# Re-ordering the head of a one-core kernel: x tile 0 in two loads, weights ahead of x tile 2, copies in halves, and the filler matmuls re-cut

## The chip, the cores and the metric

The kernel runs on one core of a Trainium2 chip. The metric is the device time in microseconds (us) of one execution; lower is better. A run's *span*, from the first to the last instruction in the trace, is about 1.4 us shorter than its time. One of the runs of the kernel before took 2341 us and is left out everywhere. The experiments ran in three groups of four on three different chips (a1 to b1, c1 to c4, d1 to d4), each beside runs of the kernel before on the same chip.

PE is the matmul engine (PEld its weight loads), DVE is VectorE, ACT ScalarE, POOL GpSimd, SP the engine that issues most loads. In these traces each engine executes its instructions in the order in which the program gives them to it, and one that waits holds up those behind it.

## The reference, cut to what matters

```python
xn = layernorm(x)                       # x: 2048 x 1024
h  = xn @ w1 + b1                       # 1024 -> 3584
act = h * tanh(softplus(h))
y_B = act @ w2                          # 3584 -> 1024
# y_A: a diagonal complex recurrence over the 2048 rows:
# projection in (B), scan, projection out (C), skip (Dskip)
return x + y_A + y_B
```

The kernel handles 2048 rows in four blocks of 512, each of four *x tiles* of 128 rows. Nothing can be multiplied before x is normalised and transposed. In the first block that is done tile by tile: statistics, square root, scaling, transposes on PE into PSUM (the banks to which PE writes its results), copies from PSUM into `xnT`. Then the first six output tiles of the dense layer are computed in two halves of 256 rows (`first_half`), so that PE can start when only tiles 0 and 1 are ready. Everything up to there is "the head" below.

## The kernel before

The parts that the change and the argument touch. First the loads and their order; ring slots are 512 KB pieces of `w1`, in pieces of 512 bytes:

```python
for q in range(NQ):
    load_x(SP, 0, q)                      # four x tiles, 256 KB each
for src, r0, n in ((A_log_dt, ...), (A_Lambda_im, ...), (A_Lambda_re, ...), (B_b1, ...)):
    AC.dma(... st[r0:r0 + n, :] ...)      # the parameters: 13 KB in four small loads, ScalarE's queue
for i in range(NRING):
    ring_load()                           # weights, SP's queue
    if i == 3:
        SP.dma(... dsk ...)
```

Then the head itself. `keep_busy` issues filler matmuls whose result nobody reads; they are there for the PE clock.

```python
keep_busy(76)
for q in range(2):                        # VectorE: statistics of tiles 0 and 1
    first_sums_v(q, 0); first_sums_v(q, 1); first_var_v(q)
first_sqrt(0)                             # ScalarE
first_mean_a(2)                           # ScalarE: sums of tile 2, ahead of tile 1's root
first_sqrt(1)
first_var_a(2); first_sqrt(2)
first_apply(0); first_transpose(0); keep_busy(4)
first_apply(1); first_transpose(1); keep_busy(4)
first_copy(0, VE)
first_copy(1, VE, 0, 4); first_copy(1, AC, 4, NK)
# ... tile 3's sums and root on ScalarE, first_apply(2), first_apply(3) ...
for f in range(NSPLIT):
    first_half(f, 0)
    if f == 0:                            # the parameter transpose, and its copy
        PE.op(... transpose(ps16(5)[:, 0:NST], st[:, :], ident[0:NST, 0:NST]) ...)
        vop(... tensor_copy(par[:, :], ps16(5)[:, 0:NST]) ...)
    if f in (2, 3):
        first_transpose(f); first_copy(f, VE)
```

Of the kernel before, what the change touches and what calls it, by code (L numbers as in the profile page):

```python
# [5 lines left out]
ALU = mybir.AluOpType  # L6
# [3 lines left out]
P = 128  # L10
# [146 lines left out]
def build_kernel(nc, A_x, A_Lambda_re, A_Lambda_im, A_B_re, A_B_im, A_C_re, A_C_im,  # L157
                 A_log_dt, A_Dskip, B_w1, B_b1, B_w2, out):
    bf16, f32, i32 = DT.bfloat16, DT.float32, DT.int32
    S, D = A_x.shape[1], A_x.shape[2]  # L160
# [4 lines left out]
    NQ = TB // P  # L165
    NK = D // P
# [8 lines left out]
    PE = Queue(nc, "pe")  # L175
    VE = Queue(nc, "ve")
    AC = Queue(nc, "ac")
    PO = Queue(nc, "po")
    SP = Queue(nc, "sp")

    def sb(name, shape, dtype):
        return nc.alloc_sbuf_tensor(name, shape, dtype)
# [4 lines left out]
    b_ring = [Buf("ring%d" % i) for i in range(NRING)]  # L187
# [16 lines left out]
    b_xnT = [Buf("xnT%d" % q, parts=[Buf("xnT%d_%d" % (q, h)) for h in range(2)]) for q in range(NQ)]  # L204
# [3 lines left out]
    xx = sb("xx", [P, 2, NQ, D], bf16)  # L208
    b_xx = [[Buf("xx%d_%d" % (i, q), parts=[Buf("xx%d_%d_%d" % (i, q, h)) for h in range(2)])
             for q in range(NQ)] for i in range(2)]  # L210
# [7 lines left out]
    NST = 3 * NJ + NF  # L218
    st = sb("st", [NST, P], bf16)
    b_st = Buf("st")  # L220
    ident = sb("ident", [P, P], bf16)
    b_ident = Buf("ident")
    par = sb("par", [P, NST], f32)
    b_par = Buf("par")
    stats = sb("stats", [P, 2, 2, 6], f32)
    b_stats = [Buf("stats%d" % i) for i in range(2)]
# [21 lines left out]
    ps = nc.alloc_psum_tensor("ps", [P, 8, TB], f32)  # L248
    b_ps = [Buf("ps%d" % i) for i in range(8)]

    def ps16(i):
        return ps[:, i, :].bitcast(bf16)
# [23 lines left out]
    vop, aop, pop = VE.op, AC.op, PO.op  # L276
# [7 lines left out]
    def load_x(queue, blk, q):  # L284
        r0 = blk * TB + q * P
        i = blk % 2
        queue.dma(lambda e: e.dma_start(xx[:, i, q, :], A_x[0, r0:r0 + P, :]),  # L287
                  s_xx[i][q] if blk else s_x0[q], writes=[b_xx[i][q]])

    for q in range(NQ):  # L290
        load_x(SP, 0, q)
    for src, r0, n in ((A_log_dt, 2 * NJ, NJ), (A_Lambda_im, NJ, NJ), (A_Lambda_re, 0, NJ),
                       (B_b1, 3 * NJ, NF)):
        AC.dma(lambda e, src=src, r0=r0, n=n: e.dma_start(
# [8 lines left out]
    def ring_load():  # L303
        i = n_loaded[0]
        if i >= len(items):
            return
        n_loaded[0] += 1
        kind, g = items[i]
        s = i % NRING
        if kind == "w1":  # L310
            dst = ring[:, s, :].rearrange("p (k f) -> p k f", k=NK)
            src = B_w1[:, g * 256:(g + 1) * 256].rearrange("(k p) f -> p k f", p=P)
        else:
            dst = ring[:, s, :].rearrange("p (f d) -> p f d", f=2)
            src = B_w2[g * 256:(g + 1) * 256, :].rearrange("(f p) d -> p f d", p=P)
        SP.dma(lambda e: e.dma_start(dst, src), s_ring[s], writes=[b_ring[s]])

    for i in range(NRING):
        ring_load()
        if i == 3:  # L320
            SP.dma(lambda e: e.dma_start(dsk[:], A_Dskip.partition_broadcast(P)), s_dsk, writes=[b_dsk])


# [12 lines left out]
    def rc(q, n):  # L336
        return rs[:, q, n:n + 1]

    def first_sums_v(q, h):
        s = q % 2  # L340
        vop(lambda e: e.bn_stats(stats[:, s, h, :], xx[:, 0, q, h * 512:(h + 1) * 512]),
            reads=[b_xx[0][q]], writes=[b_stats[s]])

    def first_var_v(q):
        s = q % 2
        vop(lambda e: e.bn_aggr(mv[:, q, :], stats[:, s, :, :]), reads=[b_stats[s]], writes=[b_mv[q]])

    def first_mean_a(q):
        aop(lambda e: e.activation(sq[:], xx[:, 0, q, :], AF.Identity, bias=kon[:, 1:2], accum_out=rc(q, 3)),
            reads=[b_xx[0][q], b_kon], writes=[b_sq, b_rs[q]])  # L350
        aop(lambda e: e.activation(mv[:, q, 0:1], rc(q, 3), AF.Copy, scale=-1.0 / D),
            reads=[b_rs[q]], writes=[b_mv[q]])

    def first_var_a(q):
        aop(lambda e: e.activation(sq[:], xx[:, 0, q, :], AF.Square, bias=mv[:, q, 0:1], accum_out=mv[:, q, 1:2]),
            reads=[b_xx[0][q], b_mv[q]], writes=[b_sq, b_mv[q]])

    def first_sqrt(q):
        scale = 1.0 if q < 2 else 1.0 / D
        aop(lambda e: e.activation(rc(q, 1), mv[:, q, 1:2], AF.Sqrt, scale=scale, bias=kon[:, 2:3]),  # L360
            reads=[b_mv[q], b_kon], writes=[b_rs1[q]])

    def first_apply(q):
        y = rc(q, 1)
        vop(lambda e: e.reciprocal(y, y), reads=[b_rs1[q]], writes=[b_rs1[q]])
        vop(lambda e: e.tensor_scalar(xn[:, q, :], xx[:, 0, q, :], mv[:, q, 0:1], y,
                                      op0=ALU.subtract if q < 2 else ALU.add, op1=ALU.mult),
            reads=[b_xx[0][q], b_mv[q], b_rs1[q]], writes=[b_xn[q]])

    def bank_T(q, k):  # L370
        if q == 1 and k >= NK // 2:
            return 5
        return 6 + q % 2

    def first_transpose(q):
        for k in range(NK):
            bank = bank_T(q, k)
            PE.mm(lambda e, k=k, bank=bank: e.transpose(ps16(bank)[:, k * P:(k + 1) * P],  # L378
                                                        xn[:, q, k * P:(k + 1) * P], ident[:]),
                  reads=[b_xn[q], b_ident], writes=[b_ps[bank]],  # L380
                  first=k == 0 or bank != bank_T(q, k - 1), last=k == NK - 1 or bank != bank_T(q, k + 1))

    def first_copy(q, queue, k0=0, k1=NK):
        dst = xnT[:, k0:k1, q * P:(q + 1) * P]
        bank = bank_T(q, k0)
        srcp = ps16(bank).rearrange("p (k t) -> p k t", k=NK)[:, k0:k1, :]
        b_dst = b_xnT[q] if k1 - k0 == NK else b_xnT[q].parts[k0 // 4]
        if queue is AC:
            aop(lambda e: e.copy(dst, srcp), reads=[b_ps[bank]], writes=[b_dst])  # L389
        else:  # L390
            vop(lambda e: e.tensor_copy(dst, srcp), reads=[b_ps[bank]], writes=[b_dst])
# [62 lines left out]

    def keep_busy(n):
        for i in range(n):
            PE.mm(lambda e: e.matmul(ps[:, 4, 0:P], lhsT=ident[:], rhs=ident[:], start=True, stop=True),  # L457
                  reads=[b_ident], writes=[b_ps[4]], first=i == 0, last=i == n - 1)

    keep_busy(76)  # L460
    aop(lambda e: e.activation(rs[:, :, 3], kon[:, 2:3].to_broadcast([P, NQ]), AF.Sqrt), reads=[b_kon], writes=b_rs)
    for q in range(2):
        first_sums_v(q, 0)
        first_sums_v(q, 1)
        first_var_v(q)
    first_sqrt(0)
    first_mean_a(2)
    first_sqrt(1)
    first_var_a(2)
    first_sqrt(2)  # L470
    first_apply(0)
    first_transpose(0)
    keep_busy(4)
    first_apply(1)
    first_transpose(1)
    keep_busy(4)
    first_copy(0, VE)
    first_copy(1, VE, 0, 4)
    first_copy(1, AC, 4, NK)
    first_mean_a(3)  # L480
    first_var_a(3)
    first_sqrt(3)
    first_apply(2)
    first_apply(3)
    NSPLIT = 6

    def first_half(f, half):
        s, fi = f // 2, f % 2
        wt = ring[:, s, :].rearrange("p (k f) -> p k f", k=NK)
        ts = slice(half * 256, half * 256 + 256)  # L490
        for k in range(NK):
            PE.mm(lambda e, k=k: e.matmul(ps[:, f, ts], lhsT=wt[:, k, fi * P:(fi + 1) * P], rhs=xnT[:, k, ts],  # L492
                                          start=k == 0, stop=k == NK - 1),
                  reads=[b_ring[s]] + b_xnT[2 * half:2 * half + 2], writes=[b_ps[f]],
                  first=half == 0 and k == 0, last=half == 1 and k == NK - 1)

    for f in range(NSPLIT):
        first_half(f, 0)
        if f == 0:
            PE.op(lambda e: e.transpose(ps16(5)[:, 0:NST], st[:, :], ident[0:NST, 0:NST]),  # L500
                  reads=[b_st, b_ident], writes=[b_ps[5]])
            vop(lambda e: e.tensor_copy(par[:, :], ps16(5)[:, 0:NST]), reads=[b_ps[5]], writes=[b_par])
        if f in (2, 3):
            q = f
            first_transpose(q)
            first_copy(q, VE)

# [345 lines left out]
```

## Time and profile before

| | before |
|---|---|
| first three runs | 623.45, 623.82 us (and the one of 2341 us) |
| span of the profiled run | 622.6 us |
| PE busy | 617.8 us, 99% |
| first real matmul | 10.40 us |
| first 512-column matmul (the head is over) | 21.90 us (its weight load) |
| PE's waits after the first real matmul | 0.3 us in one |

The page of the kernel before, its first line of engine times and the two lines of the chain of waits that ended last (share of the span by engine, then by line):

```profile
PE 617.8 (99%) x2981; PEld 289.3 (46%) x2981; DVE 464.5 (75%) x684; ACT 246.7 (40%) x162; POOL 50.2 (8%) x47
...
PE 99%; DVE 0%; ACT 0%; POOL 0%; issue 0%; POOLq 0%
PE ps L715 48%; PE ps L638 29%; PE ps L658 18%; PE ps L492 2%; PE ps L457 1%; DVE mt L663 0%; PE ps L378 0%; DVE xx L752 0%; ACT xnT L389 0%; POOL ident L325 0%; POOL ident L324 0%; PE ps L500 0%; POOL kon L328 0%; POOLq L838 0%
```

PE is the limit. L457 is the filler, L378 the transposes, L492 the split sums, L500 the parameter transpose. A matmul record's busy time says little of its rate, as matmuls overlap (a filler record lasts 0.22 us, and the next starts 0.06 us after it); what counts is the start of one against the start of the next.

The list of waits of PE, whole kernel (who waited for whom: total us, times, longest):

```profile
PE ps L457 <- POOL kon L328: 1.4, 1, 1.4
PE ps L492 <- ACT xnT L389: 0.5, 1, 0.5
PE ps L715 <- DVE mt L663: 0.3, 1, 0.3
```

After 10.4 us PE waits once, for 0.3 us by this list. So a shorter head should shift everything behind it, and nothing else in the kernel is to be had this way.

The timeline of the head before (start, duration, engine, line, operation, count; in brackets the idle time before and what ended it):

```profile
1.41 7.11 PE L457 MATMUL ps<-ident 128*128 128x128 bf16 x76 [1.41 <-POOL kon L328]
...
3.65 1.42 DVE L341 BATCH_NORM_STATS2 stats<-xx 128x6 f32<-128x512 bf16 x2 [3.65 <-DMA xx<-in_A_x_dram]
...
5.78 1.15 ACT L349 ACTIVATE sq<-xx,kon 128x1024 bf16<-128x1024 bf16 x1
...
6.91 0.55 DVE L366 TENSOR_SCALAR xn<-xx,mv,rs 128x1024 bf16<-128x1024 bf16 x1
...
7.67 0.55 DVE L366 TENSOR_SCALAR xn<-xx,mv,rs 128x1024 bf16<-128x1024 bf16 x1
...
8.36 0.61 PE L378 MATMUL ps<-ident,xn 128*128 128x128 bf16 x8
...
10.40 1.03 PE L492 MATMUL ps<-xnT,ring 128*128 128x256 bf16 x8 [0.54 <-ACT xnT L389]
11.37 0.20 PE L500 MATMUL ps<-ident,st 52*128 52x52 bf16 x1
```

Tile 0 is normalised at 7.46 us, but PE is in its filler until 8.36. The filler's starts lie 107 ns apart up to 7.05 us and 56 ns from there on: the clock was released (went from half rate to full) at about 7.1 us. The parameter transpose stands behind eight real matmuls, at 11.37 us; the trace's landing records have the last parameter at 5.38 us, so it had 6 us to spare.

### The profile page before, as it was taken

Reading aid. Unit: us, or ns where it says so; the run is one execution under the profiler, and the core shown is the slowest. Engines: PE = TensorE matmul, PEld = TensorE weight load, DVE = VectorE, ACT = ScalarE, POOL = GpSimd, SP = SyncE. Lnnn points to the kernel's source line nnn. Section 1 sums busy time; section 2 is a strip of 40 time slices with the busy share of each in tenths; the row PEclk is TensorE's granted clock in tenths of the full one; section 3 lists DMA queues with packets and bytes.
Section 4 is the critical chain, followed back from the end, with each engine's and each line's share of the span. In section 5 each row is a group of like instructions: output and inputs, shape, how many; then the busy total and the mean of one; then the engine's idle time right before and its main releaser. Section 6 shows DMA issues by size and latency. Waiting matters only on the chain.

```text
span 622.6 us, 7430 instructions
## 1 busy us (share of the span) xinstructions
PE 617.8 (99%) x2981; PEld 289.3 (46%) x2981; DVE 464.5 (75%) x684; ACT 246.7 (40%) x162; POOL 50.2 (8%) x47
## 2 busy tenths in 40 slices
PE   8999999999999999999999999999999999999998
PEld 8644444444444444444444444444444444444443
DVE  4799999999557599998047759999624856999603
ACT  6679996332069950000008992000000999000000
POOL 1899000000100000000010000000000000000000
DMA  9999976750364400864055420285204541033001
GB/s 265 230 274 272 221 142 187 192 164 1 123 188 161 136 0 18 228 172 125 17 186 148 157 103 0 76 222 158 87 34 136 156 149 68 0 126 111 1 0 68
DMA packets 124188, 79.41 MB, mean 128 GB/s; under 512 B 48890, under 2 KB 106490, under 8 KB 124154
## 3 DMA queue, kind: packets, MB, share of 16 engines
q1 hardware_dynamic: 120656, 71.58, 42.2%
q10 hardware_dynamic: 2538, 4.21, 1.8%
q0 software_dynamic: 960, 3.15, 1.6%
q8 instruction: 24, 0.39, 0.3%
q14 instruction: 10, 0.08, 0.0%
HBM read 63.19 MB, written 4.19 MB: 108 GB/s over the span
## 4 chain that ended last, share of the span: by engine, by line
PE 99%; DVE 0%; ACT 0%; POOL 0%; issue 0%; POOLq 0%
PE ps L715 48%; PE ps L638 29%; PE ps L658 18%; PE ps L492 2%; PE ps L457 1%; DVE mt L663 0%; PE ps L378 0%; DVE xx L752 0%; ACT xnT L389 0%; POOL ident L325 0%; POOL ident L324 0%; PE ps L500 0%; POOL kon L328 0%; POOLq L838 0%
## 5 line engine op out<-in xcount | busy, mean ns | idle before, releaser
L715 PE MATMUL ps<-ring,act 128*128 128x512 bf16 x896 | 194.2, 379 | 0.3 <-DVE mt L663 0.3
L638 PE MATMUL ps<-xnT,ring 128*128 128x512 bf16 x848 | 183.7, 379 | 0.0
L616 ACT ACTIVATE act<-hb 128x3584 bf16<-128x3584 bf16 x16 | 50.9, 3183 | 245.5 <-DVE hb L645 245.0
L715 PEld LDWEIGHTS ps<-ring,act 128*128 128x128 bf16 x896 | 87.6, 98 | 106.3 <-DVE mt L663 0.8
L638 PEld LDWEIGHTS ps<-xnT,ring 128*128 128x128 bf16 x848 | 83.0, 98 | 99.8
L645 DVE TENSOR_SCALAR hb<-ps,par 128x512 bf16<-128x512 f32 x112 | 82.9, 748 | 56.2 <-PE ps L638 54.3
L715 PE MATMUL ps<-CT,hT 128*128 128x512 bf16 x512 | 111.2, 379 | 0.0
L658 PE MATMUL ps<-xnT,BT 128*128 128x512 bf16 x512 | 111.2, 379 | 0.0
L663 DVE TENSOR_TENSOR mt<-ps,tab 128x1024 bf16<-128x1024 f32 x64 | 75.4, 1220 | 13.3 <-PE ps L658 11.7
L715 PEld LDWEIGHTS ps<-CT,hT 128*128 128x128 bf16 x512 | 50.1, 98 | 60.4
L658 PEld LDWEIGHTS ps<-xnT,BT 128*128 128x128 bf16 x512 | 50.1, 98 | 60.4
L752 DVE TENSOR_TENSOR xx<-ps,xx 128x1024 bf16<-128x1024 f32 (+1 forms) x17 | 19.5, 1161 | 70.1 <-PE ps L715 70.0
L681 DVE TENSOR_TENSOR_SCAN hT<-cs,qi,hT 128x512 bf16<-128x512 f32 x48 | 58.9, 1270 | 0.0
L618 ACT ACTIVATE act<-act 128x3584 bf16<-128x3584 bf16 x16 | 51.0, 3191 | 0.2
L617 ACT ACTIVATE act<-act 128x3584 bf16<-128x3584 bf16 x16 | 51.0, 3190 | 0.2
L686 DVE TENSOR_TENSOR mt<-hT,tab 128x1024 bf16<-128x1024 bf16 x64 | 41.4, 689 | 1.1
L623 DVE TENSOR_TENSOR act<-act,hb 128x3584 bf16<-128x3584 bf16 x16 | 32.9, 2059 | 1.3 <-ACT act L618 1.3
L287 POOL DMA_DIRECT2D xx<-in_A_x_dram x12 | 6.7, 558 | 254.0 <-DVE xx L752 250.1
L592 ACT ACTIVATE ct<-CT,cs 128x512 f32<-128x512 bf16 x16 | 11.5, 718 | 28.8 <-DVE CT L594 24.5
L617 ACT ACT_TABLE_LOAD x16 | 20.5, 1283 | 0.3
L618 ACT ACT_TABLE_LOAD x16 | 20.5, 1283 | 0.3
L681 DVE TENSOR_TENSOR_SCAN hT<-cs,hT 128x512 bf16<-128x512 f32 x16 | 18.7, 1209 | 0.0
(78 smaller groups left out, 280.4 us busy)
## 6 DMA issues: line engine op xcount, KB each, us to landing
ring<-in_B_w_dram SPq DMA_DIRECT2D x112, 512.0 KB, 3.7
out_dram<-xx ACTq DMA_DIRECT2D x15, 256.0 KB, 2.0
xx<-in_A_x_dram POOLq DMA_DIRECT2D x12, 256.0 KB, 4.2
xx<-in_A_x_dram SPq DMA_DIRECT2D x4, 256.0 KB, 3.5
dsk<-in_A_Dskip_dram SPq DMA_DIRECT2D x1, 256.0 KB, 6.3
out_dram<-xx ACTq DMA_DIRECT2D x2, 128.0 KB, 1.7
xnT<-xn SPq DMA_TRANSPOSE x12, 4.5
BT<-in_A_B_re_dram SPq DMA_TRANSPOSE x8, 5.7
```

The lines of the kernel that those rows point to most:

```text
L616: aop(lambda e: e.activation(a, hs, AF.Exp), reads=[b_hb[g % 2]], writes=[b_act[g]])
L617: aop(lambda e: e.activation(a, a, AF.Ln, bias=1.0), reads=[b_act[g]], writes=[b_act[g]])
L618: aop(lambda e: e.activation(a, a, AF.Tanh), reads=[b_act[g]], writes=[b_act[g]])
L623: vop(lambda e: e.tensor_tensor(a, a, hs, op=ALU.mult), reads=[b_act[g], b_hb[g % 2]], writes=[b_act[g]])
L638: PE.mm(lambda e, k=k: e.matmul(ps[:, bank, :], lhsT=wt[:, k, fi * P:(fi + 1) * P], rhs=xnT[:, k, :], start=k == 0, stop=k == NK - 1), rea ...
L645: vop(lambda e: e.tensor_scalar(hb[:, hs, :], ps[:, bank, :], b1(f), None, op0=ALU.add), reads=[b_ps[bank], b_par], writes=[b_hbf[hs]])
L658: PE.mm(lambda e, j=j, ci=ci, k=k, bank=bank: e.matmul(ps[:, bank + ci, :], lhsT=BT[:, ci, j, k, :], rhs=xnT[:, k, :], start=k == 0, stop= ...
L663: vop(lambda e, s=s, u=u, j=j: e.tensor_tensor(mt[:, s, :, :], u, tab[:, s, j, :].unsqueeze(1).to_broadcast([P, 2, TB]), op=ALU.mult), rea ...
L681: vop(lambda e, ci=ci, init=init: e.tensor_tensor_scan(out=hT[:, ci, j, :], data0=cj("r", j).to_broadcast([P, TB]), data1=hT[:, ci, j, :], ...
L686: vop(lambda e, s=s: e.tensor_tensor(mt[:, s, :, :], hT[:, :, j, :], tab[:, s, j, :].unsqueeze(1).to_broadcast([P, 2, TB]), op=ALU.mult), ...
L715: PE.mm(lambda e: e.matmul(ps[:, u, :], lhsT=lhsT, rhs=rhs, start=st_, stop=last), reads=reads, writes=[b_ps[u]], first=st_, last=last)
L752: vop(lambda e: e.tensor_tensor(xr, src, xr, op=ALU.add), reads=b_src + [b_x], writes=[b_x])
```

## The change

The intent is to start the first real matmul sooner: tile 0 in two loads so that statistics start on the first half; the first weights ahead of x tiles 2 and 3; tile 2's statistics moved from ScalarE to VectorE so that nothing stands before tile 1's root; copies of both tiles in halves on two engines out of four PSUM banks; and less filler, with the parameter transpose put into it.

```diff
--- before.py
+++ after.py
@@ -287,8 +287,10 @@
         queue.dma(lambda e: e.dma_start(xx[:, i, q, :], A_x[0, r0:r0 + P, :]),
                   s_xx[i][q] if blk else s_x0[q], writes=[b_xx[i][q]])
 
-    for q in range(NQ):
-        load_x(SP, 0, q)
+    for h in range(2):
+        SP.dma(lambda e, h=h: e.dma_start(xx[:, 0, 0, h * 512:(h + 1) * 512], A_x[0, 0:P, h * 512:(h + 1) * 512]),
+               DmaSem(nc, "d_x00_%d" % h), writes=[b_xx[0][0].parts[h]])
+    load_x(SP, 0, 1)
     for src, r0, n in ((A_log_dt, 2 * NJ, NJ), (A_Lambda_im, NJ, NJ), (A_Lambda_re, 0, NJ),
                        (B_b1, 3 * NJ, NF)):
         AC.dma(lambda e, src=src, r0=r0, n=n: e.dma_start(
@@ -317,7 +319,10 @@
 
     for i in range(NRING):
         ring_load()
-        if i == 3:
+        if i == 0:
+            load_x(SP, 0, 2)
+            load_x(SP, 0, 3)
+        if i == 5:
             SP.dma(lambda e: e.dma_start(dsk[:], A_Dskip.partition_broadcast(P)), s_dsk, writes=[b_dsk])
 
 
@@ -339,7 +344,7 @@
     def first_sums_v(q, h):
         s = q % 2
         vop(lambda e: e.bn_stats(stats[:, s, h, :], xx[:, 0, q, h * 512:(h + 1) * 512]),
-            reads=[b_xx[0][q]], writes=[b_stats[s]])
+            reads=[b_xx[0][q].parts[h]], writes=[b_stats[s]])
 
     def first_var_v(q):
         s = q % 2
@@ -356,7 +361,7 @@
             reads=[b_xx[0][q], b_mv[q]], writes=[b_sq, b_mv[q]])
 
     def first_sqrt(q):
-        scale = 1.0 if q < 2 else 1.0 / D
+        scale = 1.0 if q < 3 else 1.0 / D
         aop(lambda e: e.activation(rc(q, 1), mv[:, q, 1:2], AF.Sqrt, scale=scale, bias=kon[:, 2:3]),
             reads=[b_mv[q], b_kon], writes=[b_rs1[q]])
 
@@ -364,12 +369,12 @@
         y = rc(q, 1)
         vop(lambda e: e.reciprocal(y, y), reads=[b_rs1[q]], writes=[b_rs1[q]])
         vop(lambda e: e.tensor_scalar(xn[:, q, :], xx[:, 0, q, :], mv[:, q, 0:1], y,
-                                      op0=ALU.subtract if q < 2 else ALU.add, op1=ALU.mult),
+                                      op0=ALU.subtract if q < 3 else ALU.add, op1=ALU.mult),
             reads=[b_xx[0][q], b_mv[q], b_rs1[q]], writes=[b_xn[q]])
 
     def bank_T(q, k):
-        if q == 1 and k >= NK // 2:
-            return 5
+        if q < 2 and k >= NK // 2:
+            return 4 + q
         return 6 + q % 2
 
     def first_transpose(q):
@@ -454,30 +459,35 @@
 
     def keep_busy(n):
         for i in range(n):
-            PE.mm(lambda e: e.matmul(ps[:, 4, 0:P], lhsT=ident[:], rhs=ident[:], start=True, stop=True),
-                  reads=[b_ident], writes=[b_ps[4]], first=i == 0, last=i == n - 1)
-
-    keep_busy(76)
+            PE.mm(lambda e: e.matmul(ps[:, 3, 0:P], lhsT=ident[:], rhs=ident[:], start=True, stop=True),
+                  reads=[b_ident], writes=[b_ps[3]], first=i == 0, last=i == n - 1)
+
+    keep_busy(44)
     aop(lambda e: e.activation(rs[:, :, 3], kon[:, 2:3].to_broadcast([P, NQ]), AF.Sqrt), reads=[b_kon], writes=b_rs)
+    PE.op(lambda e: e.transpose(ps16(2)[:, 0:NST], st[:, :], ident[0:NST, 0:NST]),
+          reads=[b_st, b_ident], writes=[b_ps[2]])
+    keep_busy(12)
     for q in range(2):
         first_sums_v(q, 0)
         first_sums_v(q, 1)
         first_var_v(q)
-    first_sqrt(0)
-    first_mean_a(2)
-    first_sqrt(1)
-    first_var_a(2)
-    first_sqrt(2)
+        first_sqrt(q)
     first_apply(0)
     first_transpose(0)
     keep_busy(4)
     first_apply(1)
     first_transpose(1)
     keep_busy(4)
-    first_copy(0, VE)
+    first_copy(0, VE, 0, 4)
     first_copy(1, VE, 0, 4)
+    first_copy(0, AC, 4, NK)
     first_copy(1, AC, 4, NK)
     first_mean_a(3)
+    vop(lambda e: e.tensor_copy(par[:, :], ps16(2)[:, 0:NST]), reads=[b_ps[2]], writes=[b_par])
+    for h in range(2):
+        first_sums_v(2, h)
+    first_var_v(2)
+    first_sqrt(2)
     first_var_a(3)
     first_sqrt(3)
     first_apply(2)
@@ -491,17 +501,13 @@
         for k in range(NK):
             PE.mm(lambda e, k=k: e.matmul(ps[:, f, ts], lhsT=wt[:, k, fi * P:(fi + 1) * P], rhs=xnT[:, k, ts],
                                           start=k == 0, stop=k == NK - 1),
-                  reads=[b_ring[s]] + b_xnT[2 * half:2 * half + 2], writes=[b_ps[f]],
+                  reads=[b_ring[s]] + [b.parts[k // 4] for b in b_xnT[2 * half:2 * half + 2]], writes=[b_ps[f]],
                   first=half == 0 and k == 0, last=half == 1 and k == NK - 1)
 
     for f in range(NSPLIT):
         first_half(f, 0)
-        if f == 0:
-            PE.op(lambda e: e.transpose(ps16(5)[:, 0:NST], st[:, :], ident[0:NST, 0:NST]),
-                  reads=[b_st, b_ident], writes=[b_ps[5]])
-            vop(lambda e: e.tensor_copy(par[:, :], ps16(5)[:, 0:NST]), reads=[b_ps[5]], writes=[b_par])
-        if f in (2, 3):
-            q = f
+        if f in (2, 4):
+            q = 1 + f // 2
             first_transpose(q)
             first_copy(q, VE)
 
```

## The prediction

> **What bounds the kernel now.** PE. The page gives PE 617.8 us of a 622.6 us span (99%), and the chain of waits that ended last is 99% PE, nearly all in four matmul groups that the change does not touch. In the list of waits PE, once its first real matmul has run, waits 0.3 us in the rest of the kernel. So only the head can be won: the timeline has the first real matmul (256 columns, first tile of the dense layer) at 10.40 us, and all later work follows rigidly.
>
> **The head before (timeline).** x tile 0 is complete at 3.62 us; VectorE statistics of tile 0 run 3.65 to 5.3, of tile 1 5.23 to 6.84; tile 0 is normalised at 7.46, tile 1 at 8.22 because its square root waited behind ScalarE's 1.15 us sum of tile 2. PE's 76 filler matmuls hold it until 8.35, 0.9 us after tile 0 was ready. Then transposes (0.45 us a tile) and copies of 0.69 and 0.41 us on VectorE and 0.59 on ScalarE, finishing 10.27. After the first 8 real matmuls the parameter transpose costs PE 0.22 us.
>
> **The change, costed.**
> 1. Half of tile 0 lands about 0.6 us sooner (estimate: half the data of a load whose packets ran 1.8 to 3.1 us), so the two 0.69 us statistics start at about 3.0 and tile 0 is applied by 6.8, not 7.46; tile 1, its root no longer behind ScalarE's sums, by 7.45, not 8.22.
> 2. Filler: 44+12 and the parameter transpose in place of 76. Its spacing is 107 ns until 7.05 us and 56 ns after. 44 end at 6.1, the rest at about 7.3: PE is free 1.0 us sooner. The parameter transpose's 0.22 us leaves the chain; the parameters had landed by 5.4, so it should not stall.
> 3. Copies in four halves (0.40 VectorE, 0.59 ScalarE): the last ends at about 9.3, and the first four matmuls start before it. First real matmul at about 8.9 (−1.5).
> 4. Weights: loads move about 290 GB/s, so ring slot 0 lands at about 6.3 in place of 8.74, but x tiles 2 and 3 stand before slot 1, which still lands at about 10.5: wanted at 10.7, it just fits.
> 5. Tile 2's statistics go to VectorE (1.4+0.2 us, from about 9.0), so it is ready at about 11.7, when PE wants to transpose it: 0 to 0.3 us of stall. Tile 3's last copy comes only 0.9 us before its use: 0 to 0.1 us.
>
> Sum: the second halves of the sums start at about 15.3 in place of 16.76. The end moves by about −1.4 us.
>
> **Predicted time 622.4 us**, 8 times in 10 between 621.7 and 623.4. Faster by over 2% (12.5 us): 0.005, as the whole head is 10.4 us. Within 2%: 0.99. Slower by over 2%: 0.005.
>
> **What would show it.** First real matmul at 8.6 to 9.3; tile 0 applied by 6.9; PE waits under 0.5 us in all between 9 and 16 us; from 30 us on nothing but the shift.
>
> **What would make it wrong.** The clock. The Trainium skill, "TensorE: Matmul & The Clock Gate", Part 1, says that PE runs at half rate until one window of about 3.4 us was busy, and that the window runs free of the kernel. This trace agrees: 5.6 us of filler before the spacing halved. If a gap at the parameter transpose, or after the shorter filler, spoils a window, transposes and first sums run at half rate to about 10.5 us and most of the gain is lost. Second: ring slot 1 later than 10.7. Third: tile 2 later than thought.

## The result, and the profile after

The median of the first six runs was 622.83 us against 623.70 for the kernel before. The ratio, which is the mean time of the fast runs of one over that of the other's of the same rounds and so not quite the ratio of the medians, was 0.9992 with a 95% interval from 0.9968 to 1.0017. By the 2% rule that is the same speed.

But the six runs are 621.68, 621.84, 622.03, 623.63, 623.75 and 625.40 us, where five of before lie between 623.00 and 623.82. With the two repetitions below there are 16 runs of the changed kernel, mean 622.78, lowest 621.68, five of them at 623.2 and over; and 34 fast runs of before, mean 623.61, lowest 623.00, highest 624.43. The mean moved by 0.83 us, the lowest by 1.32, and the spread grew. (Of the three groups of runs of the changed kernel only the last, d3, has an interval that leaves out a ratio of 1: that the mean is lower is clear on one chip.) Two questions follow: is the gain the one that was predicted, and what takes it back in some runs?

The profiled run of the changed kernel (621.84 us, span 620.4) is one of the good ones. Its page:

```profile
PE 613.4 (99%) x2905; PEld 287.6 (46%) x2961; DVE 465.6 (75%) x687; ACT 244.7 (39%) x158; POOL 49.9 (8%) x47
```

56 matmul records are missing from this trace (2905 against 2961 weight loads), and its chain of waits wanders off PE for that reason, so the chain is not used here and later PE times are taken from the weight loads, which are complete. PE's waits, whole kernel:

```profile
PE ps L462 <- POOL kon L333: 1.4, 1, 1.4
PE ps L502 <- DVE par L486: 0.2, 1, 0.2
```

(The 0.2 us is put down to the small parameter copy that came last by the profile; the matmul needs the tile copies just ahead of it on VectorE and ScalarE.) PE's timeline in the head:

```profile
1.41 4.87 PE L462 MATMUL ps<-ident 128*128 128x128 bf16 x44 [1.41 <-POOL kon L333]
6.22 0.22 PE L467 MATMUL ps<-ident,st 52*128 52x52 bf16 x1
6.37 0.89 PE L462 MATMUL ps<-ident 128*128 128x128 bf16 x12
7.10 0.61 PE L383 MATMUL ps<-ident,xn 128*128 128x128 bf16 x8
...
8.76 2.78 PE L502 MATMUL ps<-xnT,ring 128*128 128x256 bf16 x24 [0.16 <-DVE par L486]
11.47 0.62 PE L383 MATMUL ps<-ident,xn 128*128 128x128 bf16 x8
```

and VectorE's:

```profile
2.95 1.50 DVE L346 BATCH_NORM_STATS2 stats<-xx 128x6 f32<-128x512 bf16 x2 [2.95 <-DMA xx<-in_A_x_dram]
...
4.61 1.40 DVE L346 BATCH_NORM_STATS2 stats<-xx 128x6 f32<-128x512 bf16 x2
...
6.31 0.55 DVE L371 TENSOR_SCALAR xn<-xx,mv,rs 128x1024 bf16<-128x1024 bf16 x1
...
6.96 0.55 DVE L371 TENSOR_SCALAR xn<-xx,mv,rs 128x1024 bf16<-128x1024 bf16 x1
```

The head went as forecast: tile 0 applied at 6.85 us (forecast 6.8), first real matmul at 8.76 (8.9), the first 512-column weight load at 20.21 in place of 21.90, so −1.69 us.

The span, however, fell by 2.2 us. (The trace of before is of a run of 624.02 us, 0.4 above the mean of its kernel, and this one is 0.9 below the mean of its own; the means differ by 0.83.) Laid side by side in order, the weight loads of the two traces keep a distance of 1.69 us from the end of the head to 93 us, and 2.16 to 2.19 us from there to the end. The remaining 0.5 us is one wait: the start of the first block's closing stage, where PE takes over PSUM banks that VectorE has to read first. The timeline before, then after, at that place:

```profile
93.69 4.21 PEld L715 LDWEIGHTS ps<-ring,act 128*128 128x128 bf16 x21 [0.79 <-DVE mt L663]
```

```profile
91.50 4.46 PEld L721 LDWEIGHTS ps<-ring,act 128*128 128x128 bf16 x22 [0.29 <-DVE mt L669]
```

So at this one place VectorE, not PE, sets the pace: it is busy for nearly all of the time from 30 us to the end of the first block, and it had moved by 2.2 us where PE had moved by 1.7. The profile shows where the extra comes from only in part: single VectorE operations, small ones above all, last very differently in the two traces while GpSimd runs beside them. Two operations on 8 columns, before and then after:

```profile
30.25 1.31 POOL L522 TENSOR_TENSOR ph_h<-px,py 128x512 f32<-128x512 f32 x1
30.45 1.20 DVE L451 TENSOR_SCALAR cs<-cs 128x8 f32<-128x8 f32 x2
```

```profile
28.77 0.54 DVE L456 TENSOR_SCALAR cs<-cs 128x8 f32<-128x8 f32 x2
```

The first of the pair took 1.13 us before, ending when the GpSimd operation ended, and 0.53 us after, again ending with a GpSimd operation (29.29 and 29.27 us); others of its kind take 0.17. The Trainium skill, "SBUF — State Buffer", section "Who interferes with whom", says that VectorE and GpSimd share one port pair as an exclusive lock, which a VectorE operation of this kind (`tensor_scalar`) can take, and that the later one blocks for the whole instruction; this pair of lines agrees with it. Such differences have both signs (from −1.1 to +1.1 us) and, counted by the ends of the operations from 29 us to the end of the first block, sum to 0.5 us less after the change. That the head's new order brings this about, and not the PE shift, the other traces make likely: the wait of PE at that place was 0.67 us in the kernel before and 0.71 in a variant of it (b1 below), and 0.16 to 0.20 in eleven of the twelve traces of the changed kernel and its variants, whether their head ended at 20.2 or at 23.1 us. (The twelfth, c2, had 1.05, because VectorE waited 0.8 us for an x tile of the second block.)

### The profile page after: what moved, and what is told of

The parts are those of the page before. It is cut to its first block, busy times and chain, and to the rows that moved or that the text cites. A ratio compares the mean times of both kernels' runs of the same rounds, so it can differ in the third digit from the quotient of the medians.

```text
span 620.4 us, 7332 instructions
## 1 busy us (share of the span) xinstructions
PE 613.4 (99%) x2905; PEld 287.6 (46%) x2961; DVE 465.6 (75%) x687; ACT 244.7 (39%) x158; POOL 49.9 (8%) x47
## 4 chain that ended last, share of the span: by engine, by line
PE 96%; ACT 2%; DVE 1%; issue 1%; POOL 0%; DVEq 0%; POOLq 0%
PE ps L721 49%; PE ps L644 26%; PE ps L664 18%; PE ps L502 2%; PE ps L462 1%; ACT act L624 1%; ACT act L622 1%; ACT act L623 1%; DVE hb L651 0%; DVE act L629 0%; PE ps L383 0%; ACT L623 0%; DVE xx L436 0%; DVE xx L758 0%; DVE mt L434 0%
## 5 line engine op out<-in xcount | busy, mean ns | idle before, releaser
L669 DVE TENSOR_TENSOR mt<-ps,tab 128x1024 bf16<-128x1024 f32 x64 | 75.3, 1219 | 13.3 <-PE ps L664 11.7
```

Of the source, the lines that this page charges most:

```text
L669: vop(lambda e, s=s, u=u, j=j: e.tensor_tensor(mt[:, s, :, :], u, tab[:, s, j, :].unsqueeze(1).to_broadcast([P, 2, TB]), op=ALU.mult), rea ...
```

## The experiments

Theories for the slow runs of the changed kernel:

- **Clock phase.** PE starts at half rate and is released at the end of a window of 3.4 us that runs free of the kernel (c4's record below shows such a window). With less filler, some phases lose a window.
- **Late loads.** The change takes the slack from loads: a load that lands late in some runs now stops an engine that must go on in order. Candidates: x tile 1 (wanted at 4.6 us now, at 5.2 before), ring slot 1, and the parameters (their transpose moved from 11.37 to 6.2 us on PE).
- **VectorE and GpSimd, or memory**, later in the kernel.

What the traces show of the head, in us from the start of the span; landings are the last landing record of each load, the clock is the time of its release as the records or the halved spacing show it:

| trace (its time) | parameters landed | x tile 1 landed | ring slot 1 landed | clock released | first transpose | first real matmul | tile 2 transposed |
|---|---|---|---|---|---|---|---|
| before (624.02) | 5.38 | 4.24 | 10.55 | 7.1 | 8.35 | 10.40 | 13.25 |
| the change (621.84) | 4.73 | 4.55 | 10.05 | 6.5 | 7.09 | 8.76 | 11.47 |
| a1 (621.89) | 4.69 | 4.78 | 10.23 | 5.7 | 7.14 | 8.82 | 11.53 |
| a2 (622.48) | 4.54 | 4.41 | 10.51 | 5.3 | 7.70 | 9.37 | 12.08 |
| a3 (622.57) | 4.95 | 5.45 | 10.59 | 6.1 | 7.80 | 9.47 | 12.21 |
| b1 (623.22) | 5.38 | 4.52 | 10.07 | 4.1 | 7.38 | 9.60 | 12.45 |
| c1 (622.30) | 4.61 | 4.53 | 10.99 | 4.3 | 6.88 | 9.22 | 11.92 |
| c2 (622.94) | 6.14 | 4.18 | 10.70 | 7.0 | 7.34 | 9.00 | 11.71 |
| c3 (623.35) | 4.83 | 4.69 | 9.94 | 11.7 | 7.04 | 9.11 | 12.98 |
| c4 (624.74) | 7.69 | 3.95 | 10.06 | 4.2, lost 7.65 to 11.07 | 9.15 | 11.67 | 14.38 |
| d1 (621.97) | 5.00 | 4.84 | 9.81 | 6.6 | 7.20 | 8.88 | 11.61 |
| d2 (622.54) | 8.08 | 4.03 | 10.93 | 7.3 | 7.79 | 9.46 | 12.19 |
| d3 (622.20) | 4.70 | 4.52 | 10.89 | 5.3 | 6.88 | 8.55 | 11.82 |
| d4 (621.88) | 4.47 | 4.46 | 10.51 | 4.3 | 6.96 | 8.79 | 11.50 |

### a1: the changed kernel again

No edit.

> The changed kernel again, to see how its runs fall. Its first six ran 621.7 to 622.0 (three), 623.6 and 623.8, and 625.4, while five of before lay within 0.8 us. Theory (clock phase): the levels differ by the phase of the window that releases the PE clock; a window lost costs half of 3.4 us, so levels near 621.9, 623.6 and 625.3, three groups 1.7 us apart, and a trace of a slow one shows 213 ns between 256-column matmuls. Rival (VectorE against GpSimd, or memory): a spread without steps, and a slow trace with warm matmuls (109 ns) but a later stage lengthened after 25 us.

Measured: 621.89, 622.45, 622.71, 623.21, 624.62 us; ratio 0.9990 (0.9977 to 1.0004). The spread is there again, but there are no steps of 1.7 us. The trace is a good run's, so it shows no slow head.

### a2: the change with 76 filler matmuls

```diff
-    keep_busy(12)
+    keep_busy(32)
```

> The change with 44+32 filler matmuls, 76 in all as before, all else as changed. Clock phase: filler lasts until 8 to 9 us in every phase, so every run is warm by 8.3; the levels at 623.6 and 625.4 vanish, all runs within 1 us of each other; floor about 0.5 to 1.0 us higher than the changed kernel's fast level since the first transpose waits for filler: 622.3 to 623.2. Rival: spread as in the changed kernel, some runs over 623.5.

Measured: 622.48 to 623.07 us in five runs; ratio 0.9988 (0.9974 to 1.0002). The slow group is gone and the floor is 0.6 us up, as the clock theory said. But the same holds for a late x tile 1: with the filler holding the first transpose until 7.70 us, that tile may land 0.8 us late without anyone noticing. The run does not separate the two.

### a3: the parameter transpose out of the filler

```diff
-    keep_busy(44)
+    keep_busy(57)
...
-    PE.op(lambda e: e.transpose(ps16(2)[:, 0:NST], st[:, :], ident[0:NST, 0:NST]), ...)
-    keep_busy(12)
...
     first_transpose(1)
+    PE.op(lambda e: e.transpose(ps16(2)[:, 0:NST], st[:, :], ident[0:NST, 0:NST]), ...)
     keep_busy(4)
```

> The change with 57 filler matmuls in one piece and the parameter transpose moved behind tile 1's transposes. Tells the two forms of the clock theory apart. If the 0.2 us gap at the parameter transpose spoils the window: fast runs only, 621.6 to 622.2. If the filler is simply too short (57 matmuls end by 7.5 us, where the slowest phase needs 8.2): slow runs as often as in the changed kernel.

Measured: 622.05, 622.26, 622.53, 622.57, 623.88 us; ratio 0.9985 (0.9973 to 0.9998). Neither outcome: one slow run of five. The trace gave what was not asked for. VectorE's waits in the first 9 us:

```profile
DVE stats L346 <- DMA xx<-in_A_x_dram: 3.7, 2, 3.0
```

Two waits, not one: 3.0 us for tile 0 and 0.7 us for tile 1, which landed at 5.45 us, and the first transpose came at 7.80, not 7.1 (VectorE's program has tile 1's statistics ahead of the scaling of tile 0), long after the clock was released (6.1 us). So a late x tile 1 does go straight into the head, by 0.7 us here. Before, the statistics of tile 1 began at 5.23 us: the change had used up the slack of that load.

### b1: the kernel before with 57 filler matmuls

```diff
-    keep_busy(76)
+    keep_busy(57)
```

> The kernel before with 57 filler matmuls for 76, nothing else. Clock phase: before loses its steadiness: its best runs 0.5 to 0.8 us under 623.6 (first transpose at 7.5 in place of 8.35), its worst 1.7 us or more above it, 625 to 626. Rival: 623.0 to 623.8 as before, no slow group.

Measured: 623.22, 623.30, 623.36, 623.69, 624.56 us; ratio 1.0001 (0.9988 to 1.0013). In its trace the first transpose is 1.0 us earlier than before and the last weight load 0.8 us earlier, yet the mean does not move, and one run is 1 us over the rest. A miss for both theories as I had put them. Less filler alone earns nothing that five runs of this kernel show. PE's timeline:

```profile
1.42 4.61 PE L457 MATMUL ps<-ident 128*128 128x128 bf16 x57 [1.42 <-POOL kon L328]
7.39 0.62 PE L378 MATMUL ps<-ident,xn 128*128 128x128 bf16 x8 [1.36 <-DVE xn L366]
```

The earlier transpose in this trace is not the work of the 19 matmuls taken out. The clock was released at 4.1 us here and at 7.1 in the trace of before; by an estimate from the 56 ns spacing, 19 more would have ended at about 6.9 us, still ahead of tile 0, which was ready at 7.33. How much the filler holds PE up thus depends on when the clock is released in a run (see point 2 below).

### c1: the loads in the old order

```diff
-    load_x(SP, 0, 1)
+    for q in range(1, NQ):
+        load_x(SP, 0, q)
...
-        if i == 0:
-            load_x(SP, 0, 2)
-            load_x(SP, 0, 3)
-        if i == 5:
+        if i == 3:
```

> The change with the loads in the old order: x tiles 1, 2, 3, then the weights. Landing theory: x tile 1 has no slack in the changed kernel (it landed at 4.41 to 5.45 us, where VectorE wants it at 4.6) because ring slot 0 with its 512-byte pieces comes right behind it; with x tile 2 behind it, it lands by 4.4, the first statistics of tile 1 start at 4.6, and the slow runs vanish (all runs 621.6 to 622.8; ring slot 0 lands at 8.7, which is just when it is wanted, so the floor stays). Clock theory: the spread stays, some runs over 623.2.

Measured: 622.30, 622.30, 622.58, 622.62, 622.86 us; ratio 0.9983 (0.9970 to 0.9996). No slow run, as the landing theory said. The floor is not where it said: PE waited for the weights.

```profile
PE ps L500 <- DMA ring<-in_B_w_dram: 0.8, 1, 0.8
```

The first real matmul came at 9.22 us, 0.46 after the changed kernel's, since ring slot 0 landed at 9.18. That is the value of the new load order in a good run. In this trace x tile 1 landed at 4.53 us, no earlier than in the changed kernel; five steady runs speak for the old order, but the trace does not show that tile 1 is what it steadies.

### c2: x tile 0 in one load

```diff
-    for h in range(2):
-        SP.dma(... A_x[0, 0:P, h * 512:(h + 1) * 512] ...)
+    load_x(SP, 0, 0)
```

> The change with x tile 0 in one load. Both: statistics start at 3.6 and tile 0 is applied at about 7.5, 0.6 us later, floor 622.3 to 622.6. Landing theory: tile 1 is then wanted at 5.2 and has 0.7 us of slack, so the spread shrinks to under 1 us. Clock theory: spread as in the changed kernel, up to 624 and over.

Measured: 622.13, 622.38, 622.53, 622.94, 624.16 us; ratio 0.9987 (0.9975 to 0.9999). The first transpose came 0.25 us later than in the changed kernel, not 0.6, because the whole tile landed at 3.37 us here, against 3.62 in the trace of before, and because in the changed kernel's trace the filler held PE for 0.24 us after tile 0 was ready. The slow run is still there though tile 1 now has slack (0.8 us in the trace), so tile 1 is probably not the only cause; the slow run itself was not traced. And in this trace the parameters landed at 6.14 us: the parameter transpose, which had 1.5 us in hand in the trace of the changed kernel, had less than 0.1. It lost nothing yet: the profile puts 0.2 us of waiting down to the parameters, but the transpose started 0.25 us after the filler matmul before it, and 0.24 in the changed kernel, where they had long landed.

### c3: no filler

All `keep_busy` calls of the changed kernel taken out.

> The change without any filler matmul, to measure what a cold clock costs. Clock theory: transposes start at about 6.9 as now but at 107 ns, the sums at 213 ns for 3.4 to 6.8 us after the first, so 1.7 to 3.5 us plus the slower transposes: 624 to 626, all runs above 623.7. If the clock does not matter: 621.8 to 622.5, as PE then never holds a transpose up.

Measured: 622.90 to 623.68 us in five runs; ratio 0.9993 (0.9981 to 1.0005). The clock matters, but for less than forecast, since the release came at 11.7 us: the split sums ran 213 ns apart for 2.5 us and 109 ns after that. PE's timeline:

```profile
4.88 0.22 PE L466 MATMUL ps<-ident,st 52*128 52x52 bf16 x1 [4.88 <-DMA st<-in_B_b_dram]
7.05 1.89 PE L383 MATMUL ps<-ident,xn 128*128 128x128 bf16 x16 [1.94 <-DVE xn L371]
9.12 4.03 PE L498 MATMUL ps<-xnT,ring 128*128 128x256 bf16 x24 [0.18 <-DVE par L482]
```

Tile 2's transposes start at 12.98 us against 11.47 in the changed kernel: 1.5 us for the whole filler. And its slowest run is below three of the changed kernel's: a kernel without filler, which is cold for longer, is steadier than the changed one was in its first two groups (on other chips). That speaks against a lost window as the cause of runs at 624 and 625 us, which would then lie above this.

### c4: x tile 1 from ScalarE's queue

```diff
-    load_x(SP, 0, 1)
+    load_x(AC, 0, 1)
```

> The change with x tile 1's load issued from ScalarE's queue, ahead of the parameters, at 0.8 us in place of 1.7. Landing theory: tile 1 lands by 4.2 in every run, the slow runs vanish, all runs 621.6 to 622.6. Clock theory: spread stays, some runs over 623.2. The parameters land about 0.5 us later, still before PE wants them at 6.1.

Measured: 622.64, 622.75, 623.37, 624.02, 624.64, 624.74 us; ratio 1.0001 (0.9989 to 1.0012). Tile 1 landed early (3.95 us) and the runs became worse. This time the profiled run is the slowest of all, and it shows why. PE's waits, whole kernel:

```profile
PE ps L467 <- DMA st<-in_B_b_dram: 2.4, 1, 2.4
PE ps L462 <- POOL kon L333: 1.4, 1, 1.4
```

and PE's timeline:

```profile
1.42 3.96 PE L462 MATMUL ps<-ident 128*128 128x128 bf16 x44 [1.42 <-POOL kon L333]
7.74 0.22 PE L467 MATMUL ps<-ident,st 52*128 52x52 bf16 x1 [2.37 <-DMA st<-in_B_b_dram]
7.90 1.46 PE L462 MATMUL ps<-ident 128*128 128x128 bf16 x12
9.15 1.06 PE L383 MATMUL ps<-ident,xn 128*128 128x128 bf16 x8
...
11.67 1.03 PE L502 MATMUL ps<-xnT,ring 128*128 128x256 bf16 x8
```

The parameters, 13 KB behind x tile 1 on their queue, landed at 7.69 us. PE stood for 2.4 us at a transpose that nothing urgent needs, with tile 0 ready since 7.57 and 12 filler matmuls still to come behind it. Then the clock lapsed as well. In the table of four windows (PE busy, ..., the granted clock third from the right):

```profile
0.83:4.24 3.41, 2.82 (x27) 2.83 (x28) 0.54 (x1) 1.37 (x2) 1.83 (x7) 1.00 0.63 204
4.24:7.65 3.41, 1.14 (x20) 0.96 (x17) 3.16 (x9) 0.71 (x3) 0.00 (x0) 1.00 1.07 337
7.65:11.07 3.42, 3.33 (x31) 3.28 (x32) 0.97 (x2) 0.59 (x1) 0.00 (x0) 0.50 1.19 293
11.07:14.48 3.41, 3.31 (x34) 2.70 (x33) 2.75 (x7) 3.06 (x6) 0.00 (x0) 1.00 1.20 290
```

(The record of 1.00 for the first row stands for "nothing recorded": the filler's starts were 107 ns apart until 4.2 us.) PE was busy for a third of the window from 4.24 to 7.65 us, and at its end the clock was halved for exactly one window of 3.413 us; filler and transposes ran 107 ns apart until 11.07. The Trainium skill, "TensorE: Matmul & The Clock Gate", Part 1, "What's actually happening", gives 3413 ns for the window; the record agrees. So the clock is in it, but as the second step: a late small load stops PE, and the stop costs the clock.

### d2: c4 with the parameter transpose behind tile 1's transposes

c4's edit and a3's edit together.

> The run with x tile 1 on ScalarE's queue again (622.6 to 624.7; its trace had PE waiting 2.4 us for the parameters, landed at 7.7), with one difference: the parameter transpose behind tile 1's transposes. Theory (PE held by the parameters): the runs over 623.2 vanish, 622.2 to 622.8; the parameters still land late, at 6 to 8 us, but nobody waits. Rival (clock phase, or x tiles late): the spread stays, 2 us.

Measured: 622.46, 622.48, 622.53, 622.54, 622.62 us; ratio 0.9982 (0.9970 to 0.9995). In its trace the parameters landed even later than in c4, at 8.08 us, and nobody waited:

```profile
1.41 6.15 PE L462 MATMUL ps<-ident 128*128 128x128 bf16 x57 [1.41 <-POOL kon L333]
7.79 0.62 PE L383 MATMUL ps<-ident,xn 128*128 128x128 bf16 x8 [0.23 <-DVE xn L371]
...
9.02 0.20 PE L477 MATMUL ps<-ident,st 52*128 52x52 bf16 x1
```

The range fell from 2.1 to 0.16 us with the place of one 52-column transpose. c4 and d2 ran on different chips, and the changed kernel itself was steadier on d2's (see d3), so the ranges alone would not prove it; the two traces do, since the same late landing stops PE for 2.4 us in one and not at all in the other. The floor is higher than the changed kernel's because the first half of tile 0, which now shares the start with tile 1, landed at 3.83 us in place of 2.92.

### d1: the parameter transpose behind tile 1's transposes, and x tile 2 ahead of the weights

a3's edit, and:

```diff
     load_x(SP, 0, 1)
+    load_x(SP, 0, 2)
...
         if i == 0:
-            load_x(SP, 0, 2)
             load_x(SP, 0, 3)
```

> The change with both suspected risks taken out: the parameter transpose behind tile 1's transposes (57 filler matmuls in one piece), and x tile 2 loaded ahead of ring slot 0, so that large pieces and not the 512-byte ones follow x tile 1. Theory (late small loads on PE's and VectorE's ordered paths make the slow runs): all five within 0.8 us, 621.6 to 622.4, which would beat both kernels. Rival (clock phase alone): one or two of five above 623.2, as in the changed kernel.

Measured: 621.79, 621.93, 621.97, 622.02 and 622.76 us; ratio 0.9975 (0.9963 to 0.9988). The floor of the changed kernel, without a run over 623.2; one run lies outside the range that was expected (622.4, all within 0.8 us). It beats the kernel before. Whether it beats the changed kernel is not shown: on this chip that one was steady too.

### d3: the changed kernel once more

No edit.

> The changed kernel once more, for more of its runs and, with luck, the trace of a slow one. Theory: of five, about two over 623.0; if the profiled run is one of them, PE waits over 0.5 us for the parameters at the parameter transpose, or VectorE for x tile 1, and a cold clock follows. Clock phase alone: a slow trace with neither wait, but 107 ns between transposes.

Measured: 621.91, 622.20, 622.29, 622.37, 622.49 us; ratio 0.9978 (0.9964 to 0.9992). No slow run on this chip, so no trace of one. Its mean, 622.25, is 0.16 us above d1's 622.09, within the spread of either. Its trace shows the third load without slack:

```profile
PE ps L502 <- DMA ring<-in_B_w_dram: 0.5, 1, 0.5
```

Ring slot 1 landed at 10.89 us, where this run, with its first real matmul at 8.55, wanted it at 10.3. The earlier start was given back at once.

### d4: tile 0's copy in one piece

```diff
-        if q < 2 and k >= NK // 2:
-            return 4 + q
+        if q == 1 and k >= NK // 2:
+            return 5
...
-    first_copy(0, VE, 0, 4)
+    first_copy(0, VE)
...
-    first_copy(0, AC, 4, NK)
```

> The change with tile 0's transposed copy in one piece of 0.69 us on VectorE, as before. If the halves are worth what I costed: tile 1's first half is copied 0.3 us later, first real matmul 0.1 to 0.4 us later than with halves and the best run 0.1 to 0.4 us later; if ScalarE's half of tile 1 is what ends last, nothing changes.

Measured: 621.84, 621.88, 622.10, 622.50 us; ratio 0.9975 (0.9961 to 0.9989). From tile 1's first transpose to the first real matmul it took 1.15 us, against 1.00 in the three traces of the changed kernel. So the halves of tile 0 are worth 0.15 us in the trace and nothing that the times show.

## Why the prediction was right or wrong, point by point

The forecast of 622.4 us, 8 times in 10 between 621.7 and 623.4, holds the median of 622.83. Of the 16 runs of the changed kernel, 11 lie in the range, one a hair below it and four above.

1. **Half of tile 0 first: right.** Statistics began at 2.95 us (forecast 3.0), tile 0 was applied at 6.85 (6.8), tile 1 at 7.51 (7.45). The part that belongs to the half load is smaller than 0.6 us: c2 lost only 0.25 us in the trace without it.
2. **Filler: right on time in this trace, unsafe on the parameters.** The first transpose came at 7.09 us (7.3). The step that proved unsafe is "the parameters had landed by 5.4, so it should not stall". One landing time of one trace was taken for the landing time. The twelve traces in which the parameters are loaded at the same moment have them landed at 4.5 to 6.1 us, and the latest (c2) left less than 0.1 us; issued 0.45 us later (c4, d2) they landed at 7.7 and 8.1, and in c4 PE waited 2.4 us and lost the clock for a window. No trace of the changed kernel itself shows the stall: in all three they landed at 4.7 us. "PE is free 1.0 us sooner" rests on one trace too, one in which the clock was released late (7.1 us; 4.1 to 7.3 in the thirteen traces with filler). An estimate from the measured spacings (107 ns before the release, 56 after) ends the 76 matmuls at 8.4 us for a release at 7.1 and at 6.9 for one at 4.1; in the second case tile 0, ready at 7.46, is not held at all. Part of the gain is then missing in runs with an early release, which fits b1 and the spread of before (623.0 to 624.4, this trace's run at 624.02), but was not tested.
3. **Copies in halves: right.** The first real matmul came at 8.76 us (8.9). But the halves are not what brings it: undoing tile 0's (d4) costs 0.15 us.
4. **Weights: right, with no reserve.** Slot 0 landed at 6.57 us (6.3), slot 1 at 10.05 (10.5). The old order costs 0.46 us in the trace (c1). The warning about slot 1 came true in d3, for 0.5 us.
5. **Tile 2 and tile 3: right.** Tile 2's transposes started at 11.47 us after a wait of under 0.1 us, and the weight loads lost under 0.1 us waiting for tile 3's copy.
6. **"The end moves by about −1.4 us": the head moved by −1.69, the profiled run by −2.2, the mean by −0.83.** Two terms were missing from the sum. VectorE sets the start of the first block's closing stage, and −0.5 us came from there; "from 30 us on nothing but the shift" was wrong by that. And the runs spread, those of before too: 0.4 us of the difference between −2.2 and −0.83 is that the traced run of before was slower than its mean, 0.9 that the traced run of the changed kernel was faster than its own. That the median lies in the range is therefore partly luck: the head gained more than forecast in the trace, and slow runs of unknown cause took it back.
7. **The clock: the warning named the wrong link.** No trace with filler lost a window to the phase: in all thirteen the release came between 4.1 and 7.3 us, ahead of the first transpose. What can spoil the window is a stop of PE in the midst of the filler, as in c4.

What stays open: no slow run of the changed kernel itself fell into a profile. That late parameters (c4), a late x tile 1 (a3) and a late ring slot 1 (d3) each cost time in a head of this form is shown, and so is a cost behind the head, which leaves the third theory open: in c2 a late x tile of the second block cost 0.85 us at the closing stage; in which proportion they make the runs at 623.2 to 625.4 us is not. Nor is why a3, b1 and c2 have one slow run of five each, or why one chip had none in nine runs of the changed kernel and d4. Why the parameters land late is argued only: they are 256-byte pieces among the x and weight loads, and the Trainium skill, "DMA: Bandwidth & Descriptors", section "Issuing engines are not separate DMA queues", says that loads from any issuing engine interleave on the same 16 DMA engines. Their landings from 4.5 to 8.1 us fit that, but no run took the other loads away.

## What to carry to other kernels

When a change moves an instruction forward on an engine that executes in order, ask when its operand lands in the worst run and not in the profiled one: a tiny load that nobody needs urgently can hold up everything behind it. Put such work where there is already idle time behind the urgent work (the parameter transpose behind tile 1's transposes cost PE nothing that the trace shows and had 3.4 us of reserve in d1). After tightening a head, look at the spread of the runs as well as at the median, since slack taken out of a load's landing can come back as variation (x tile 1 landed between 4.41 and 5.45 us in the traces that issue it at the same moment, behind two halves of tile 0, and was wanted at 4.6). And read a head from more than one trace: in the thirteen with filler the clock was released anywhere from 4.1 to 7.3 us.

## What the Trainium skill lacked or had wrong

- "TensorE: Matmul & The Clock Gate", Part 1, has the clock released after a window of about 3.4 us of sustained activity. A full window is not needed (windows counted back by 3.413 us from the recorded release, busy time as the trace gives it): in b1 the window that ended at 4.08 us had 2.66 us of PE work (78%) and released the clock; in d2 the one that ended at 3.89 had 2.48 us (73%) and did not.
- The same part has it halved after an idle window. In c4 a window with 1.14 us of PE work (33%) was enough to halve it; in b1 one with 2.05 us (60%) was not.
- The same page, Part 4: PE-mode transpose, says that transposes do not count as busy for the clock in the same way. In c4 the window from 7.65 to 11.07 us was half transposes (1.7 us) and half filler, and the clock was released at its end; with the filler alone it would have been 50% busy, less than d2's 73%, which was not enough.
- No page says how much the landing of small loads varies beside large ones: 13 KB of parameters issued at the same moment landed between 4.5 and 6.1 us in twelve traces.
